# Merging the column-group sums of a sliding-window attention beside a gated feed-forward

## The chip, the cores and the metric

One core of one Trainium2 chip. The metric is device time in microseconds, median of several executions; the profile is one further execution, whose span is some 1.7 us shorter than its device time. The engines are named as the profile names them: PE (TensorE matmuls), PEld (TensorE weight loads), DVE (VectorE), ACT (ScalarE), POOL (GpSimd), SP (the DMA queue's issuer).

Most executions of one kernel agree within 0.3%. Some have a mean granted TensorE clock of 0.992 or 0.993 and take 1.4 to 2.2 us more (the kernel before: 240.2 and 241.7). They widen the intervals. Where I compare single microseconds I therefore go by the medians and, more sharply, by the trace: the stretch from the start of the first projection to the start of the last gating product, which leaves out the loads at the start and the store at the end.

## The reference

```python
xn = layernorm(x)                        # x: 1 x 2048 x 512
q, k, v = split(xn @ wqkv)               # 32 heads of 16
# each position attends to 8 taps: itself and 2, 4, ... 14 positions back
logits[h, s, w] = sum_d q[h, s, d] * k[h, s - 2 w, d] / 4      # -1e9 before position 0
attn = softmax(logits, over w)
o[h, s, d] = sum_w attn[h, s, w] * v[h, s - 2 w, d]
s = o @ wo
g = silu((gelu(xn @ w_gate) * (xn @ w_up)) @ w_down)           # 512 -> 1792 -> 512
out = x + s * g
```

## The kernel before

Sequence positions go in four blocks of 512 columns. For each block TensorE does a feed-forward of 14 steps (`glu`: one gate and one up projection, 8 matmuls of 128 by 128 by 512), 12 projections for the next block (`qkv`) and four `down` steps (14 matmuls of w_down, 4 of wo). Attention runs beside them: VectorE multiplies q with shifted k (`pk`, 8 taps) and the weights with shifted v (`pv`, 8 products), and TensorE sums over partitions. These sums have only 32 output rows, so four of them stand side by side in the array's four groups of 32 columns. Their place in the program is given by hand: `at(("glu", j, 6), f, ...)` runs `f` ahead of step 6 of block j's feed-forward. A bank is the part of TensorE's output memory (PSUM) that one group of sums fills; the banks of a ring are used in turn, each again only when an engine has emptied it.

```python
mm = pool("mm", 5, space=PSUM)     # five banks, a ring for all projections
att = pool("att", 2, space=PSUM)   # two banks for the sums
trp = pool("trp", 1, space=PSUM)   # one bank for transposes

def logits(j, wh):                                  # four of the eight taps
    L = att.tile([P, TQ], F32, tag="att")
    for c in range(NC):
        for wl in range(WL):
            matmul(L[32*wl : 32*(wl+1), :], lhsT=dsum[:, c, :],          # 128 x 32
                   rhs=pk[WL*wh + wl][:, c, :], start=(c == 0), stop=(c == NC-1))
    activation(out=E[:, wh, :], in_=L, func=Exp, scale=SCALE)

def denominators(j):                                # 8 matmuls of 128 x 32, 128 columns
    ...                                             # then rs = reciprocal(den) on VectorE

def spread_reciprocals(j):                          # 4 full-array matmuls, rb = copy on ScalarE
    sp = att.tile([P, TQ], F32, tag="att")
    ...

def av_sum(j, g):                                   # one quarter of the head dimension
    o = att.tile([P, TQ], F32, tag="att")
    for wh in range(WH):
        for i in range(4):
            matmul(o[32*i : 32*(i+1), :], lhsT=hsum, rhs=pv[g, wh][:, i, :],
                   start=(wh == 0), stop=(wh == WH-1))
    tensor_tensor(out=oT[:, g, :], in0=o, in1=rb, op=mult)               # VectorE

# ... cut: the places of the first block
for j in range(1, NJ):
    at(("down", j-1, 3), logits, j, 0)
    at(("glu", j, 1), logits, j, 1)
    at(("glu", j, 2), denominators, j)
    at(("glu", j, 4), spread_reciprocals, j)
    for i in range(8):
        at(("glu", j, 2 + i), av_product, j, i // 2, i % 2)
    for g in range(NC):
        at(("glu", j, 6 + 2*g), av_sum, j, g)
```

The softmax here doesn't subtract the row's maximum and nothing guards it: scores larger than these inputs give would overflow.

## Time and profile before

| | before |
|---|---|
| device time | 240.16 us (240.11 to 240.26, 3 runs) |
| profiled span | 238.2 us |
| TensorE matmuls busy | 229.1 us, 96% of the span |
| share of the chain that ended last | PE 92%, ACT 4% |
| column-group runs (L, den, o) | 4 x (2 + 1 + 4) = 28 |
| table loads on ScalarE | 25 of 1.283 us |
| first projection to last product | 7.96 to 234.26: 226.30 us |

A table load (ACT_TABLE_LOAD) stands in ScalarE's stream wherever gelu, exponential and silu follow one another.

The page is read from the busy shares down: which engine never rests, then whether the chain that ended last is that engine's own. If both say TensorE, only what shortens TensorE's own sequence counts, or what takes away a wait of TensorE. The prediction shows the lines.

### The profile page before, as it was taken

How to read it: one execution, taken by the hardware profiler on the slowest of the kernel's cores; microseconds unless marked ns; L12 is line 12 of the kernel's file. 1: busy time of each engine (PE TensorE's matmuls, PEld its weight loads, DVE VectorE, ACT ScalarE, POOL GpSimd, SP SyncE). 2: the span in 40 equal slices, each digit the busy share in tenths (PEclk: the TensorE clock that was granted, in tenths of full speed). 3: DMA queues.
4: the chain of work that ended last, by engine and by line, in shares of the span. 5: the costliest groups of instructions: out<-in, count | busy, mean ns of one | idle time of the engine just before them, and what ended most of it. 6: DMA issues, size and time to landing. Idle time of an engine off the chain costs nothing.

```text
span 238.2 us, 3516 instructions
## 1 busy us (share of the span) xinstructions
PE 229.1 (96%) x1317; PEld 102.8 (43%) x1342; DVE 143.7 (60%) x222; ACT 150.1 (63%) x237; POOL 24.5 (10%) x80
## 2 busy tenths in 40 slices
PE   7889999999999999999999999999999999999993
PEld 2764444444444343444444444334444434434441
DVE  3559868698488269832537539951347629963131
ACT  2778889976616986568822996656651798566211
POOL 3379922300000000000000000000000000000000
PEclk9999999999999999999999999999999999999999
DMA  6999499610286300000158500000047810000001
GB/s 177 361 373 355 120 198 245 212 45 3 88 198 159 91 0 0 3 0 0 64 132 197 127 20 4 0 0 3 14 128 173 191 31 0 1 3 0 22 22 44
DMA packets 21793, 22.66 MB, mean 95 GB/s; under 512 B 1552, under 2 KB 21776, under 8 KB 21776
## 3 DMA queue, kind: packets, MB, share of 16 engines
q1 hardware_dynamic: 21488, 22.17, 34.8%
q10 hardware_dynamic: 288, 0.26, 0.4%
q8 instruction: 10, 0.16, 0.3%
q14 instruction: 7, 0.06, 0.1%
HBM read 18.22 MB, written 4.21 MB: 94 GB/s over the span
## 4 chain that ended last, share of the span: by engine, by line
PE 92%; ACT 4%; DMA 1%; DVE 1%; issue 1%; POOL 0%; DVEq 0%
PE g_ps L211 20%; PE y_ps L355 20%; PE u_ps L211 19%; PE qkv_ps L211 18%; PE s_ps L366 6%; PE o_ps L326 4%; PE L_ps L265 3%; PE tr L191 1%; ACT xnT L195 1%; DMA x_sb<-in_A_x_dram 1%; ACT ge L345 1%; ACT L345 1%; ACT u L347 0%; PE den_ps L288 0%; PE sp_ps L303 0%
## 5 line engine op out<-in xcount | busy, mean ns | idle before, releaser
L211 PE MATMUL g_ps<-xnT,wg_sb 128*128 128x512 bf16 x218 | 57.4, 380 | 0.5
L211 PE MATMUL u_ps<-xnT,wu_sb 128*128 128x512 bf16 x218 | 56.3, 379 | 0.1
L355 PE MATMUL y_ps<-wd_sb,h 128*128 128x512 bf16 x217 | 50.4, 379 | 0.5 <-issue 0.2
L349 DVE TENSOR_TENSOR h<-ge,u 128x512 bf16<-128x512 bf16 x56 | 23.6, 421 | 37.9 <-ACT u L347 37.5
L211 PE MATMUL qkv_ps<-xnT,wqkv_sb 128*128 128x512 bf16 (+1 forms) x219 | 44.2, 348 | 1.6 <-ACT xnT L195 1.3
L256 DVE TENSOR_TENSOR pk<-q_sb,k_sb 128x2048 bf16<-128x2048 bf16 x32 | 38.0, 1218 | 12.2 <-ACT k_sb L231 12.2
L345 ACT ACTIVATE ge<-g_ps 128x512 bf16<-128x512 f32 x56 | 33.7, 602 | 14.3 <-PE g_ps L211 14.2
L347 ACT ACTIVATE u<-u_ps 128x512 bf16<-128x512 f32 x56 | 33.5, 599 | 12.9 <-PE u_ps L211 11.5
L314 DVE TENSOR_TENSOR pv<-E,v_arr 128x2048 bf16<-128x2048 bf16 x32 | 38.5, 1209 | 0.0
L211 PEld LDWEIGHTS <-wu_sb 128*128 128x128 bf16 x224 | 21.9, 98 | 26.4
L355 PEld LDWEIGHTS <-h 128*128 128x128 bf16 x224 | 21.7, 98 | 27.0 <-issue 1.3
L363 ACT ACTIVATE sl<-y_ps 128x512 bf16<-128x512 f32 x16 | 9.6, 597 | 36.4 <-PE y_ps L355 36.4
L211 PEld LDWEIGHTS <-wg_sb 128*128 128x128 bf16 x224 | 19.9, 98 | 27.5 <-issue 7.2
L211 PEld LDWEIGHTS <-wqkv_sb 128*128 128x128 bf16 x224 | 21.1, 98 | 19.5 <-issue 3.3
L375 DVE TENSOR_TENSOR m<-s_ps,sl 128x512 bf16<-128x512 f32 x16 | 11.1, 692 | 29.5 <-PE s_ps L366 29.5
L366 PE MATMUL s_ps<-wo_sb,oT 128*128 128x512 bf16 x63 | 16.4, 379 | 0.1
L171 DVE BATCH_NORM_STATS2 stats<-x_sb 128x6 f32<-128x512 bf16 x16 | 10.9, 679 | 6.5 <-DMA x_sb<-in_A_x_dram 6.5
L228 ACT ACTIVATE q_sb<-qkv_ps 128x512 bf16<-128x512 f32 (+1 forms) x20 | 10.2, 511 | 4.6 <-PE qkv_ps L211 4.3
L234 ACT ACTIVATE vst<-qkv_ps 128x512 bf16<-128x512 f32 x16 | 9.6, 597 | 5.2 <-PE qkv_ps L211 4.3
L335 DVE TENSOR_TENSOR oT<-o_ps,rb 128x512 bf16<-128x512 f32 x16 | 10.9, 682 | 2.2 <-PE o_ps L326 2.2
L231 ACT ACTIVATE k_sb<-qkv_ps 128x512 bf16<-128x512 f32 (+1 forms) x20 | 10.2, 512 | 3.1 <-PE qkv_ps L211 2.8
L195 ACT ACTIVATE xnT<-tr 128x512 bf16<-128x512 bf16 x16 | 9.5, 597 | 3.7 <-PE tr L191 3.7
(42 smaller groups left out, 135.6 us busy)
## 6 DMA issues: line engine op xcount, KB each, us to landing
v_arr<-vT SPq DMA_DIRECT2D x16, 520.0 KB, 5.4
vT<-vst SPq DMA_DIRECT2D x16, 128.0 KB, 1.7
out_dram<-o_t SPq DMA_DIRECT2D x16, 128.0 KB, 1.8
wg_sb<-in_B_w_gate_dram SPq DMA_DIRECT2D x2, 896.0 KB
wu_sb<-in_B_w_up_dram SPq DMA_DIRECT2D x2, 896.0 KB, 13.1
wd_sb<-in_B_w_down_dram SPq DMA_DIRECT2D x1, 1792.0 KB, 17.4
wqkv_sb<-in_A_wqkv_dram SPq DMA_DIRECT2D x3, 512.0 KB, 6.2
x_sb<-in_A_x_dram SPq DMA_DIRECT2D x3, 512.0 KB, 10.2
```

Source lines behind the costliest of these rows:

```text
L171: nc.vector.bn_stats(out=stats[:, t, :], in_=x_sb[:, t, :])
L195: nc.scalar.activation(out=xnT[j][:, :, i * P : (i + 1) * P], in_=tr[:].rearrange("p (c n) -> p c n", c=NC), func=AF.Copy,)
L211: nc.tensor.matmul(ps[:], lhsT=w[:, dk, lo : lo + P], rhs=xnT[j][:, dk, i0 : i0 + n], start=(dk == 0), stop=(dk == NC - 1),)
L256: nc.vector.tensor_tensor(out=pk[:], in0=st[j]["q"][:], in1=k_sb[:, :, off : off + TQ], op=ALU.mult)
L314: nc.vector.tensor_tensor(out=pv[:], in0=st[j]["E"][:, wh, :].unsqueeze(1).to_broadcast([P, 4, TQ]), in1=st[j]["va"][:, 4 * g : 4 * g + 4, ...
L335: nc.vector.tensor_tensor(out=st[j]["oT"][:, g, :], in0=o[:], in1=st[j]["rb"][:], op=ALU.mult)
L345: nc.scalar.activation(out=ge[:], in_=g_ps[:], func=AF.Gelu_apprx_tanh)
L347: nc.scalar.activation(out=u[:], in_=u_ps[:], func=AF.Copy)
L349: nc.vector.tensor_tensor(out=h[:], in0=ge[:], in1=u[:], op=ALU.mult)
L355: nc.tensor.matmul(y[:], lhsT=st[j][fc][:, tt * P : (tt + 1) * P], rhs=wd_sb[:, fc, :], start=(fc == 0), stop=(fc == NF - 1),)
L366: nc.tensor.matmul(s[:], lhsT=st[j]["oT"][:, g, tt * P : (tt + 1) * P], rhs=wo_sb[:, g, :], start=(g == 0), stop=(g == NC - 1),)
L375: nc.vector.tensor_tensor(out=m[:], in0=s[:], in1=sl[:], op=ALU.mult)
```

## The change

The intent is to give TensorE fewer passages between full-array matmuls and column-group matmuls. All eight taps of the logits go in one run into two neighbouring banks, with one exponential over both; two quarters of the attention sums go in one run into two banks, with one division; the denominators go directly ahead of the first such run. For the banks, transposes and the spread reciprocals move into the general ring.

```diff
-    att = pool("att", 2, space=bass.MemoryType.PSUM)
-    trp = pool("trp", 1, space=bass.MemoryType.PSUM)
+    att = pool("att", 1, space=bass.MemoryType.PSUM)
...
-        tr = trp.tile([P, NC * P], BF16, name="tr")
+        tr = mm.tile([P, NC * P], BF16, name="tr", tag="mm")
...
-    def logits(j, wh):
-        L = att.tile([P, TQ], F32, name="L_ps", tag="att")
+    def logits(j):
+        L = att.tile([P, WH, TQ], F32, name="L_ps", tag="pair")
+        for wh in range(WH):
...
-        nc.scalar.activation(out=E[:, wh, :], in_=L[:], func=AF.Exp, scale=SCALE)
+        nc.scalar.activation(out=E[:], in_=L[:], func=AF.Exp, scale=SCALE)
...
-        den = att.tile([P, P], F32, name="den_ps", tag="att")
+        den = att.tile([P, P], F32, name="den_ps")
...
-        sp = att.tile([P, TQ], F32, name="sp_ps", tag="att")
+        sp = mm.tile([P, TQ], F32, name="sp_ps", tag="mm")
...
-    def av_sum(j, g):
+    def av_sums(j, gg):          # quarters 2*gg and 2*gg + 1, tile [P, 2, TQ], tag "pair"
+    def divide(j, gg):           # one product over [P, 2, TQ]
... (places, blocks 1 to 3; the first block likewise)
-        at(("down", j - 1, 3), logits, j, 0)
-        at(("glu", j, 1), logits, j, 1)
-        at(("glu", j, 2), denominators, j)
-        at(("glu", j, 4), spread_reciprocals, j)
+        at(("glu", j, 0), logits, j)
-        for g in range(NC):
-            at(("glu", j, 6 + 2 * g), av_sum, j, g)
+        at(("glu", j, 7), denominators, j)
+        at(("glu", j, 7), av_sums, j, 0)
+        at(("glu", j, 9), spread_reciprocals, j)
+        at(("glu", j, 9), divide, j, 0)
+        at(("glu", j, 12), av_sums, j, 1)
+        at(("glu", j, 12), divide, j, 1)
...
-            at(("qkv", j, 9 + w) if early else ("down", j - 1, w // 2), qk_product, j, w)
+            at(("qkv", j, 9 + w) if early else ("down", j - 1, w // 3), qk_product, j, w)
```

As the last two lines show, some of VectorE's products move forward as well, so that all eight taps are there for the one run; in the first block so do six of the eight `pv` products.

More of the change, by code (lines that the diff above doesn't have):

```diff
@@ L259, in qk_product @@
         st[j]["pk"][w] = pk
-    def logits(j, wh):
-        L = att.tile([P, TQ], F32, name="L_ps", tag="att")
-        for c in range(NC):
-            for wl in range(WL):
-                nc.tensor.matmul(
-                    L[H * wl : H * (wl + 1), :],
-                    lhsT=dsum[:, c, :],
-                    rhs=st[j]["pk"][WL * wh + wl][:, c, :],
-                    start=(c == 0),
-                    stop=(c == NC - 1),
-                )
-        if wh == 0:
-            st[j]["E"] = ep.tile([P, WH, TQ], BF16, name="E")
-        E = st[j]["E"]
-        nc.scalar.activation(out=E[:, wh, :], in_=L[:], func=AF.Exp, scale=SCALE)
+    def logits(j):
+        L = att.tile([P, WH, TQ], F32, name="L_ps", tag="pair")
+        for wh in range(WH):
+            for c in range(NC):
+                for wl in range(WL):
+                    nc.tensor.matmul(
+                        L[H * wl : H * (wl + 1), wh, :],
+                        lhsT=dsum[:, c, :],
+                        rhs=st[j]["pk"][WL * wh + wl][:, c, :],
+                        start=(c == 0),
+                        stop=(c == NC - 1),
+                    )
+        E = st[j]["E"] = ep.tile([P, WH, TQ], BF16, name="E")
+        nc.scalar.activation(out=E[:], in_=L[:], func=AF.Exp, scale=SCALE)
         if j == 0:
-            for wl in range(WL):
-                w = WL * wh + wl
-                if w:
-                    nc.gpsimd.memset(E[H * wl : H * (wl + 1), wh, 0 : w * DIL], 0.0)
+            for w in range(1, W):
+                wh, wl = divmod(w, WL)
+                nc.gpsimd.memset(E[H * wl : H * (wl + 1), wh, 0 : w * DIL], 0.0)
     def denominators(j):
         E = st[j]["E"]
-        den = att.tile([P, P], F32, name="den_ps", tag="att")
+        den = att.tile([P, P], F32, name="den_ps")
         for wh in range(WH):
@@ L320, in av_product @@
         st[j]["pv"][g, wh] = pv
-    def av_sum(j, g):
-        o = att.tile([P, TQ], F32, name="o_ps", tag="att")
-        for wh in range(WH):
-            for i in range(4):
-                nc.tensor.matmul(
-                    o[H * i : H * (i + 1), :],
-                    lhsT=hsum[:],
-                    rhs=st[j]["pv"][g, wh][:, i, :],
-                    start=(wh == 0),
-                    stop=(wh == WH - 1),
-                )
-        if g == 0:
+    def av_sums(j, gg):
+        o = att.tile([P, 2, TQ], F32, name="o_ps", tag="pair")
+        for g in range(2):
+            for wh in range(WH):
+                for i in range(4):
+                    nc.tensor.matmul(
+                        o[H * i : H * (i + 1), g, :],
+                        lhsT=hsum[:],
+                        rhs=st[j]["pv"][2 * gg + g, wh][:, i, :],
+                        start=(wh == 0),
+                        stop=(wh == WH - 1),
+                    )
+        st[j]["o"] = o
+    def divide(j, gg):
+        if gg == 0:
             st[j]["oT"] = op.tile([P, NC, TQ], BF16, name="oT")
         nc.vector.tensor_tensor(
-            out=st[j]["oT"][:, g, :], in0=o[:], in1=st[j]["rb"][:], op=ALU.mult
+            out=st[j]["oT"][:, 2 * gg : 2 * gg + 2, :],
+            in0=st[j]["o"][:],
+            in1=st[j]["rb"][:].unsqueeze(1).to_broadcast([P, 2, TQ]),
+            op=ALU.mult,
         )
@@ L401 @@
         at(("glu", 0, w), qk_product, 0, w)
-    at(("glu", 0, 6), logits, 0, 0)
-    at(("glu", 0, 10), logits, 0, 1)
-    at(("glu", 0, 12), denominators, 0)
+    at(("glu", 0, 9), logits, 0)
     for i in range(8):
-        at(("glu", 0, 12 + i) if i < 2 else ("qkv", 1, i), av_product, 0, i // 2, i % 2)
-    at(("qkv", 1, 0), spread_reciprocals, 0)
-    for g in range(NC):
-        at(("qkv", 1, 2 + 3 * g), av_sum, 0, g)
+        at(("glu", 0, 12 + i) if i < 2 else ("qkv", 1, (0, 1, 3, 4, 5, 6)[i - 2]),
+           av_product, 0, i // 2, i % 2)
+    at(("qkv", 1, 3), denominators, 0)
+    at(("qkv", 1, 3), av_sums, 0, 0)
+    at(("qkv", 1, 5), spread_reciprocals, 0)
+    at(("qkv", 1, 6), divide, 0, 0)
+    at(("qkv", 1, 10), av_sums, 0, 1)
+    at(("qkv", 1, 10), divide, 0, 1)
     for j in range(1, NJ):
@@ L413 @@
             early = j > 1 and w < 3
-            at(("qkv", j, 9 + w) if early else ("down", j - 1, w // 2), qk_product, j, w)
+            at(("qkv", j, 9 + w) if early else ("down", j - 1, w // 3), qk_product, j, w)
         for i in range(TPQ):
             at(("down", j - 1, i), load_v, j, [i])
-        at(("down", j - 1, 3), logits, j, 0)
-        at(("glu", j, 1), logits, j, 1)
-        at(("glu", j, 2), denominators, j)
-        at(("glu", j, 4), spread_reciprocals, j)
+        at(("glu", j, 0), logits, j)
         for i in range(8):
             at(("glu", j, 2 + i), av_product, j, i // 2, i % 2)
-        for g in range(NC):
-            at(("glu", j, 6 + 2 * g), av_sum, j, g)
+        at(("glu", j, 7), denominators, j)
[4 more added lines that the diff above has]
+        at(("glu", j, 12), divide, j, 1)
     HT = TPQ // 2
```

## The prediction

> **What bounds the kernel now.** I read the page from the top: first the busy shares and the slices, to find the engine that never rests; then the chain that ended last, to see whether that engine also sets the end; then the same chain in order of time for one stretch, to see what one run of column-group sums costs; last the timeline around those runs, to see who feeds them.
>
> ```profile
> PE 229.1 (96%) x1317; PEld 102.8 (43%) x1342; DVE 143.7 (60%) x222; ACT 150.1 (63%) x237; POOL 24.5 (10%) x80
> ...
> PE   7889999999999999999999999999999999999993
> ...
> PEclk9999999999999999999999999999999999999999
> ...
> PE 92%; ACT 4%; DMA 1%; DVE 1%; issue 1%; POOL 0%; DVEq 0%
> PE g_ps L211 20%; PE y_ps L355 20%; PE u_ps L211 19%; PE qkv_ps L211 18%; PE s_ps L366 6%; PE o_ps L326 4%; PE L_ps L265 3%; PE tr L191 1%; ACT xnT L195 1%; DMA x_sb<-in_A_x_dram 1%; ACT ge L345 1%; ACT L345 1%; ACT u L347 0%; PE den_ps L288 0%; PE sp_ps L303 0%
> ```
>
> TensorE is busy in every slice but the first three and the last, at full clock, and 92% of the chain is its own. Nothing off TensorE is worth anything unless TensorE waits for it. The attention sums (L_ps, o_ps, den_ps) are 7 to 8% of the chain, though their arithmetic should be less. The chain in order of time shows why (start, length, piece):
>
> ```profile
> 79.36 0.86 PE u_ps L211 x4
> 80.22 0.98 PE L_ps L265 x16
> 81.20 0.97 PE g_ps L211 x4
> 82.17 0.86 PE u_ps L211 x4
> 83.03 0.23 PE den_ps L288 x8
> ...
> 89.63 0.86 PE u_ps L211 x4
> 90.50 0.55 PE o_ps L326 x8
> 91.04 0.97 PE g_ps L211 x4
> 92.01 0.65 PE u_ps L211 x3
> ```
>
> A group of four full-array matmuls takes 0.86 us, 0.2155 each. A group of four right after a column-group run takes 0.97, so 0.11 more. The column-group run itself, four matmuls side by side, should take 16/4 x 0.2155 = 0.86 for L and 8/4 x 0.2155 = 0.43 for o; it shows 0.98 and 0.55, again 0.11 to 0.12 more. The timeline gives the same from start to start:
>
> ```profile
> 79.20 1.03 PE L211 MATMUL u_ps<-xnT,wu_sb 128*128 128x512 bf16 x4
> 80.15 1.05 PE L265 MATMUL L_ps<-pk,dsum 128*32 128x512 bf16 x16
> 81.13 1.04 PE L211 MATMUL g_ps<-xnT,wg_sb 128*128 128x512 bf16 x4
> 82.01 1.03 PE L211 MATMUL u_ps<-xnT,wu_sb 128*128 128x512 bf16 x4
> 82.96 0.30 PE L288 MATMUL den_ps<-E,hsum 128*32 128x128 bf16 x8
> 83.19 1.04 PE L211 MATMUL g_ps<-xnT,wg_sb 128*128 128x512 bf16 x3
> ...
> 89.47 1.03 PE L211 MATMUL u_ps<-xnT,wu_sb 128*128 128x512 bf16 x4
> 90.43 0.61 PE L326 MATMUL o_ps<-pv,hsum 128*32 128x512 bf16 x8
> 90.97 1.04 PE L211 MATMUL g_ps<-xnT,wg_sb 128*128 128x512 bf16 x4
> ```
>
> Take the start of the group ahead, add 0.86, and read to the start of the group after. L: 81.13 - 80.06 = 1.07, which is 0.86 + 0.21. o: 90.97 - 90.33 = 0.64, which is 0.43 + 0.21. den: 83.19 - 82.87 = 0.32, and its eight matmuls of 128 columns, four side by side, are 2 x 0.054 = 0.11, so 0.21 again. Three lengths, one constant: every run costs 0.21 us whatever is in it, half on entering (0.09 to 0.10), half on leaving (0.11 to 0.12).
>
> **What the Trainium skill says.** "TensorEngine Tiling (Array Packing)", section Key Properties, says that a change of the tiling mode, not of the tile, drains TensorE. The trace agrees and gives the size that the page lacks, 0.21 us for in and out together. "TensorE: Matmul & The Clock Gate", section Back-to-back issue gap, gives 512/2.4 + 2.5 = 216 ns for the isolated warm gap, and 131 ns as sustained; the trace has 215.5 in sustained streams and never 131, so I use 215.5. "ScalarE: Activation LUTs", section What ACT_TABLE_LOAD costs, gives about 1283 ns for a load and 1380 for a drain with it; the trace has 1283 and no such drain: an exponential that starts at 82.17 and lasts 0.60 is followed by a load at 82.78 and by the next gelu at 84.08. "PSUM — Partial Sum Buffer", section Specifications, gives 8 banks of 2 KiB per partition. The program before takes 5 + 2 + 1 of them, and the one after 5 + 2 (the pair) + 1 (the denominators), so the general pool keeps its five but must also serve 16 transposes and 4 spreads.
>
> **The change part by part.**
>
> 1. Runs. Before, each of the four blocks has two L runs, one den run and four o runs: 28 runs. After, one L run and two o runs, with den directly ahead of the first, in the same 128 by 32 tiling and with the same stationary matrix: 12 runs. All 1317 matmuls stay. Sixteen runs less at 0.213 (0.21, and another 0.01 to 0.02 that the first group after a run loses: 81.13 to 82.01 is 0.88 where 0.86 is usual) make 16 x 0.213 = 3.4 us. All of it lies on TensorE in stretches where TensorE never rests, so all of it shows, unless a wait fills it.
>
> 2. Transposes in the general pool. Before, the single transpose buffer makes TensorE wait twice. At the start the second tile's transpose waits 0.57 for the copy of the first; its data are ready at 6.62 (6.21 + 0.41), it runs at 6.89, so with its own bank it gains 0.2, and the first projections hang on the copy after it. In the first feed-forward block the third of the four transposes should start at 22.77 + 0.86 = 23.64 and starts at 23.96, behind a copy that ScalarE reached late because of a table load: 0.3. In the five-bank ring it takes the bank of an already emptied gelu tile (ready at 22.93). Together 0.5 us gained, less certain.
>
> 3. ScalarE. Before, 25 table loads of 1.283 us (9 + 8 + 7 + 1). After, gelu and exponential alternate once per block and silu comes once: 1 + 5 + 4 + 4 = 14. Eleven loads, 14 us of ScalarE, and half of the exponentials' fixed part go. ScalarE is not the bound; I count 0.
>
> 4. VectorE. Sixteen divisions of 682 ns become eight of at most 2 x 0.68 = 1.36 us, spread over two banks. Neutral or slightly better, worth 0 by itself.
>
> 5. Waits that the longer runs may bring. The first o run needs four products instead of two. In later blocks I walked the queue: the exponential ends about 1.1 us after the L run, a gelu load (1.28) and 0.6 follow, so the first products start some 1.3 us after step 2 begins, and products with their gate multiply go at 1.47 us each (88.94 to 90.42), faster than a step of 1.73. The fourth product is there 1.0 us before the run at step 7. The reciprocal comes behind the sixth product and is ready about 1.4 us before the spread at step 9. Second o run: 1.8 us of slack. The first block is tighter. With G the end of its L run, the chain exponential (1.0), load (1.3), gelu and copy (1.1), then VectorE without a pause (8.5 for the remaining gates, normalizations and four products, from the starts 44.50 to 50.04 less the reciprocal and the division in between) gives the fourth product at G + 12.1. TensorE gets to the o run at G + 8.65 (five steps) + 2.8 (three projections and a transpose) = G + 11.5, and to the fourth product's matmuls at G + 12.3. Slack 0.1 to 0.2, an estimate with an error as large; I put 0.1 us of loss on it.
>
> Sum: -3.4 - 0.5 + 0.1 = -3.8; from 240.16 that gives 236.4. Because part 2 is less sure than part 1, I say 236.5.
>
> **The rivals.**
>
> *A: the 0.21 belongs to the matmuls, not to the run.* Then merging saves nothing and the time is about 239.7. Against it: 8 short, 8 long and 16 long matmuls all show the same 0.21. I give it 4%.
>
> *B: a new wait eats the gain.* The first block's four products are the candidate; if my walk is off by 0.7 us, the loss is 0.5 and the time 237.0. A wait in each block, 0.3 to 0.5 us four times, would make it 238. For it: VectorE shows slices of 90% and more around the products. Against it: the reciprocal and two divisions move behind the early products, which frees about 1.5 us ahead of the first run.
>
> *C: the general pool runs dry behind the longer exponential.* After an L run TensorE fills five banks in 0.97 + 4 x 0.86 = 4.4 us; ScalarE returns the first after 1.0 + 1.28 + 0.6 = 2.9 when the exponential's table was loaded during the run, 4.2 when it was not. Before, the same count is 3.6, and no matmul waited. The slack stays positive, with 0.2 us in the worse case; a loss of 0.2 to 0.4 per block would give 237.5.
>
> *D: ScalarE's 14 us show.* Only where TensorE waits for ScalarE, and the waits list has that only for the transposes and in the start, where no load is removed. It could bring the time to 236 but hardly lower.
>
> **Range and chances.** Part 1 is a count times a constant measured three ways, good to 0.2 us; part 2 lies between 0 and 0.7 gained; part 5 between 0 and 1.3 lost. That makes 235.6 to 237.7 for eight in ten. A gain of over 2% needs 235.36 or less, 4.8 us, a microsecond beyond the sum: 6%. A loss over 2% would need 5 us of new waiting with the gain gone as well: 2%. Within 2%: 92%.
>
> **What would show each step.** Right: 12 runs, each with the same 0.21, L runs of about 1.72 + 0.11 in the chain with a following group of 0.97; the first run with den and o in one piece of about 0.97 + 0.11 without 0.11 between them; 14 table loads; the second transpose at about 6.7 us and no gap before the third in the first block; division at 1.2 to 1.4 us. TensorE's busy time then falls by about 3.4 and its idle time by up to 0.5. Wrong: "o_ps waits for pv" in the waits, over 0.5 us in total (rival B); "g_ps or u_ps waits for ge or u" right after an L run (rival C); runs that cost 0.4 (rival A). The number would be wrong first through the first block's o run, where my slack is smaller than my error.

## The result

| | before | after |
|---|---|---|
| device time, median of 6 | 240.28 us | 236.53 us (236.18 to 238.10) |
| ratio | | 0.9839 (0.9801 to 0.9877) |
| profiled span | 238.2 us | 234.4 us |
| PE busy | 229.1 us | 226.7 us |
| ACT busy | 150.1 us | 135.8 us |
| first projection to last product | 226.30 us | 7.54 to 230.45: 222.91 us |

A ratio is the mean time of one kernel's fast runs over that of the other's of the same rounds, so not quite the ratio of the medians. The median fell by 3.75 us. TensorE's busy time is no measure of it here: the trace before holds 1317 of the 1342 matmuls, that after all of them; the prediction took 1317 for the whole count, which none of its sums uses.

The page after, the same rows of the busy shares and of the chain:

```profile
PE 226.7 (97%) x1342; PEld 105.2 (45%) x1342; DVE 143.5 (61%) x214; ACT 135.8 (58%) x222; POOL 26.3 (11%) x80
...
PE 89%; DVE 4%; ACT 3%; issue 1%; DMA 1%; POOL 1%; DVEq 0%; ACTq 0%
```

Still TensorE, but VectorE now holds 4% of the chain. The chain in order of time (start, length, piece) shows the merged runs of the second block and, above them, where VectorE comes in, in the first:

```profile
47.96 2.28 DVE pv L311 x2
50.28 0.40 PE o_ps L325 x4
...
76.08 1.84 PE L_ps L265 x32
...
90.11 0.23 PE den_ps L285 x8
90.34 0.86 PE o_ps L325 x16
91.20 0.97 PE g_ps L210 x4
```

The L run of 32 matmuls takes 1.84, that is 2 x 0.86 + 0.12, where two runs of 0.98 stood. The o run behind the denominators takes 0.86, with nothing of its own for a switch: den has paid. After each run the next full-array group takes 0.97, as before. So there are 12 passages in and out instead of 28, each of the same size. The first two lines are the new wait of the first block: the last four matmuls of its o run start at 50.28, when the fourth product is done.

A second new wait is in the third block. The timeline of the changed kernel, TensorE's rows and then ScalarE's:

```profile
136.73 1.03 PE L210 MATMUL g_ps<-xnT,wg_sb 128*128 128x512 bf16 x4
137.76 1.02 PE L210 MATMUL u_ps<-xnT,wu_sb 128*128 128x512 bf16 x4
...
133.48 1.28 ACT L273 ACT_TABLE_LOAD   x1 [2.22 <-PE L_ps L265]
134.78 1.02 ACT L273 ACTIVATE E<-L_ps 128x1024 bf16<-128x1024 f32 x1
135.82 1.28 ACT L350 ACT_TABLE_LOAD   x1
137.11 0.60 ACT L350 ACTIVATE ge<-g_ps 128x512 bf16<-128x512 f32 x1
```

The up projection would start at 136.73 + 0.86 = 137.59. It starts at 137.76, because the bank it needs is the one whose gelu ends at 137.71. That gelu is late because in this block, and in this one alone, the exponential's table load itself waited for L (2.22 us) instead of running beside it.

### The profile page after: what moved, and what is told of

It reads as the page before. It is cut to its first block, busy times and chain, and to the rows that moved or that the text cites. A ratio compares the mean times of both kernels' runs of the same rounds, so it can differ in the third digit from the quotient of the medians.

```text
span 234.4 us, 3517 instructions
## 1 busy us (share of the span) xinstructions
PE 226.7 (97%) x1342; PEld 105.2 (45%) x1342; DVE 143.5 (61%) x214; ACT 135.8 (58%) x222; POOL 26.3 (11%) x80
## 4 chain that ended last, share of the span: by engine, by line
PE 89%; DVE 4%; ACT 3%; issue 1%; DMA 1%; POOL 1%; DVEq 0%; ACTq 0%
PE y_ps L360 21%; PE g_ps L210 19%; PE u_ps L210 19%; PE qkv_ps L210 17%; PE s_ps L371 6%; PE o_ps L325 3%; PE L_ps L265 2%; DVE pv L311 2%; PE tr L190 1%; DMA x_sb<-in_A_x_dram 1%; ACT ge L350 1%; DVE stats L170 1%; ACT u L352 1%; DVE h L354 1%; POOL rstd L175 1%
## 5 line engine op out<-in xcount | busy, mean ns | idle before, releaser
L210 PE MATMUL u_ps<-xnT,wu_sb 128*128 128x512 bf16 x224 | 57.5, 379 | 0.0
L360 PE MATMUL y_ps<-wd_sb,h 128*128 128x512 bf16 x224 | 51.0, 379 | 0.0
L210 PEld LDWEIGHTS <-wg_sb 128*128 128x128 bf16 x224 | 20.8, 98 | 26.6 <-issue 4.2
L337 DVE TENSOR_TENSOR oT<-o_ps,rb 128x1024 bf16<-128x1024 f32 x8 | 9.8, 1219 | 2.0 <-PE o_ps L325 2.0
```

The source lines that it names most:

```text
L210: nc.tensor.matmul(ps[:], lhsT=w[:, dk, lo : lo + P], rhs=xnT[j][:, dk, i0 : i0 + n], start=(dk == 0), stop=(dk == NC - 1),)
L360: nc.tensor.matmul(y[:], lhsT=st[j][fc][:, tt * P : (tt + 1) * P], rhs=wd_sb[:, fc, :], start=(fc == 0), stop=(fc == NF - 1),)
```

## The experiments

Ten kernels ran, each with five timed rounds against the kernel before and a profile; all gave correct results. The last two, one_run_pre and after_pre, ran on another chip than the eight before them, so they are compared with the others by the stretch and by the kernel before of their own rounds (240.18). "Stretch" is first projection to last product in the trace.

| kernel | runs of column groups | median us | ratio to before (95%) | stretch us |
|---|---|---|---|---|
| before | 28 | 240.28 | 1 | 226.30 |
| after | 12 | 236.53 | 0.984 (0.980 to 0.988) | 222.91 |
| split_all | 28 | 240.73 | 1.003 (1.000 to 1.005) | 227.07 |
| split_fine | 40 | 243.44 | 1.014 (1.011 to 1.017) | 229.71 |
| before_tr_mm | 28 | 239.97 | 1.000 (0.997 to 1.004) | 226.00 |
| late_first | 12 | 237.63 | 0.988 (0.985 to 0.991) | 222.92 |
| ins_full | 20 | 238.48 | 0.990 (0.987 to 0.994) | 224.86 |
| ins_64 | 20 | 238.70 | 0.991 (0.987 to 0.994) | 224.94 |
| ins_32 | 12 | 237.07 | 0.986 (0.982 to 0.990) | 223.25 |
| one_run | 8 | 236.58 | 0.982 (0.979 to 0.986) | 222.90 |
| one_run_pre | 8 | 235.42 | 0.980 (0.977 to 0.984) | 221.93 |
| after_pre | 12 | 236.40 | 0.985 (0.981 to 0.988) | 222.85 |

### split_all: the merged kernel with its runs cut again

```diff
-    at(("glu", 0, 9), logits, 0)
+    at(("glu", 0, 8), logits, 0, (0,)); at(("glu", 0, 9), logits, 0, (1,))
-    at(("qkv", 1, 3), denominators, 0)
-    at(("qkv", 1, 3), av_sums, 0, 0)
+    at(("qkv", 1, 1), denominators, 0); at(("qkv", 1, 2), av_sums, 0, 0, (0,))
+    at(("qkv", 1, 3), reciprocals, 0);  at(("qkv", 1, 3), av_sums, 0, 0, (1,))
... second o run of the first block: halves at qkv 9 and 10
-        at(("glu", j, 0), logits, j)
+        at(("down", j-1, 3), logits, j, (0,)); at(("glu", j, 0), logits, j, (1,))
... blocks 1 to 3: den at 5, o halves at 6 and 7, at 11 and 12; reciprocal stays at 7
```

> The changed kernel with its buffers, its single exponential, its 14 table loads and its divisions of two quarters, but with every merged run cut in two again, so that 28 column-group runs are left, each between full-array matmuls. Theory (0.21 us for each run): 236.5 + 16 x 0.213 - 0.2 (the first block's wait for the fourth product goes) = 239.7 us, 0.997 to 0.999 of the kernel before; TensorE's matmuls no fewer. Rival (the gain comes from the buffers, the table loads or the larger exponentials and divisions): 236.3 to 236.8, so 0.984.

Measured: 240.73 us. With the banks, the 14 table loads and the large exponentials and divisions of the changed kernel, cutting the runs gives the whole gain back: 227.07 - 222.91 = 4.16 us of the stretch, of which the 16 passages are 3.5 and new waits, below, the rest. So the count of runs is the cause, and the 11 saved table loads are worth nothing visible. From the first `down` step on, the three later blocks hold 12 runs more and take 235.32 - 62.61 = 172.71 us against 230.45 - 60.38 = 170.07: 2.64 us, 0.22 for each.

It lost 1.0 us more than I expected. Some 0.1 is the difference between 0.213 and 0.22; the rest lies in the first block. I had expected that block's wait for the fourth product to go (0.2 less); it grew from 0.29 to 0.65 instead (the o half starts at 51.24, the next full group at 52.44: 1.20, where the same half with its exit takes 0.55 elsewhere). The second o run waits 0.20 for the division that empties its two banks (it ends at 58.54, the run starts at 58.59), and an up projection 0.07 for a late gelu (it starts at 43.04). 3.52 - 0.29 + 0.65 + 0.20 + 0.07 = 4.15, so nothing is left over. ScalarE's rows of this kernel and of the changed one show why the first block is late:

```profile
38.76 1.28 ACT L277 ACT_TABLE_LOAD   x1
40.05 1.02 ACT L277 ACTIVATE E<-L_ps 128x1024 bf16<-128x1024 f32 x1
```

```profile
36.94 1.28 ACT L273 ACT_TABLE_LOAD   x1
38.23 1.02 ACT L273 ACTIVATE E<-L_ps 128x1024 bf16<-128x1024 f32 x1
```

The next full group starts at 38.64 in the first and at 37.69 in the second. So the exponential starts 1.41 us behind the short last half, 0.54 behind the long run: while the long run lasts, ScalarE already loads the table. A merged run hides a load that a short one does not, and everything on VectorE follows the exponential.

### split_fine: more runs yet

```diff
+        run("mid", j, fc)        # in glu, between the gate and the up projection
-        at(("glu", j, 6), av_sums, j, 0, (0,))
+        at(("glu", j, 6), av_sums, j, 0, (0,), (0,)); at(("mid", j, 6), av_sums, j, 0, (0,), (1,))
... the same for the other three halves of blocks 1 to 3
```

> As split_all, and the attention sums of blocks two to four cut once more, four matmuls to a run: 40 runs. Theory (a constant for each run, whatever is in it): 12 x 0.213 = 2.6 us more than split_all, 242.3, about 1.008 of the kernel before, and runs of four matmuls take 0.22 + 0.21 = 0.43 us from start to start. Rival (the cost grows with the work in a run): 0.0 to 1.3 us more than split_all.

Measured: 243.44 us, 2.71 more than split_all; in the stretch 229.71 - 227.07 = 2.64, again 0.22 for each of the 12 added runs. The cost is a constant for a run: a run of four matmuls pays as much as one of 32. From where its first matmul would start without a switch (90.68) to the next full group (91.11) such a run takes 0.43, as expected.

### ins_full, ins_64, ins_32: breaking a run with one matmul

```diff
         for wh in range(WH):
+            if wh == 1:
+                matmul(junk[0:COLS, :], lhsT=warm[:, 0:COLS], rhs=warm[:, 0:128])   # COLS = 128, 64, 32
             for c in range(NC):
... and the same between the two quarters of the second o run; junk shares the denominators' bank
```

> The changed kernel with one useless full-array matmul (128 by 128, 128 columns, 0.054 us of its own) in the middle of each L run and of each second o run: 8 insertions that break a run. Theory (the switch of tiling costs, not the neighbour's work): 8 x (0.22 + 0.054) = 2.2 us more than the changed kernel, 238.7. Rival (the constant belongs to the long groups ahead of and behind a run, their weight loads or their waits): 8 x 0.054 = 0.4 us more, 236.9.

> The same with 64 output columns (128 by 64, another column grouping). If a change from groups of 32 to a group of 64 counts as a change of tiling as the skill's page has it: 2.2 us more, 238.7. If all column groupings are one kind and only the whole array is another: 0.4 more, 236.9.

> Control: the same useless matmul in the tiling of the run itself (128 by 32). Both theories: 8 x 0.054 = 0.4 us at most, 236.9, in the trace no 0.1 us gaps inside the run.

The timelines of the second block's L run, first with 128 columns, then with 64:

```profile
76.65 1.05 PE L270 MATMUL L_ps<-pk,dsum 128*32 128x512 bf16 x16
77.63 0.23 PE L265 MATMUL junk<-warm 128*128 128x128 bf16 x1
77.79 1.05 PE L270 MATMUL L_ps<-pk,dsum 128*32 128x512 bf16 x16
```

```profile
76.54 1.05 PE L270 MATMUL L_ps<-pk,dsum 128*32 128x512 bf16 x16
77.52 0.24 PE L265 MATMUL junk<-warm 128*64 128x128 bf16 x1
77.69 1.05 PE L270 MATMUL L_ps<-pk,dsum 128*32 128x512 bf16 x16
```

From the start of the first half to the useless matmul are 0.98 us where the half itself takes 0.86; from it to the second half 0.16, where it takes 0.05. So 0.12 and 0.11 of switching around a single small matmul: long neighbours have no part in it. From the first `down` step on (six insertions), ins_full takes 1.65 us more than the changed kernel, 0.275 for each; ins_64 takes 1.73, 0.29; the control in the run's own tiling takes 0.29, 0.05. What is left for the switch is 0.22 to 0.24 in the first two. A change from groups of 32 to one of 64 columns costs the same as a change to the whole array. "TensorEngine Tiling (Array Packing)", section Key Properties, says that the mode, not the tile, is what drains; these three runs agree.

What the switch is made of shows in part in the weight loads (PEld). Within a tiling, a matmul's weights load while the matmul ahead of it runs: in ins_32 the useless matmul's weights start to load at 77.123, 0.214 before the matmul itself. At a change of tiling they do not. This is the load ahead of the second block's denominators in the changed kernel:

```profile
90.04 0.12 PEld L285 LDWEIGHTS <-hsum 128*32 128x32 bf16 x8 [0.42 <-issue]
```

The load starts together with its matmul, 0.309 us after the last full-array matmul (89.732) where 0.2155 is usual: 0.093 more, and one such load takes 0.093. On leaving (91.13) it is 0.096, and the load there takes 0.096. So of the 0.22 some 0.19 are as long as two weight loads that nothing hides. Whether the loads are the cost, or only wait for the same thing as the matmuls, no run here separates.

In the first block the insertion into L was largely paid by the wait there: in ins_full the run with the denominators starts at 49.87 and the next projection at 50.98, 1.11 us, with no wait left in it, and up to the first `down` step that kernel lost 0.3 us instead of 0.55.

### before_tr_mm: only the transposes moved

```diff
-    trp = pool("trp", 1, space=bass.MemoryType.PSUM)
-        tr = trp.tile([P, NC * P], BF16, name="tr")
+        tr = mm.tile([P, NC * P], BF16, name="tr", tag="mm")
```

> The kernel before with one thing of the change: transposes in the general pool of five banks, the single transpose buffer gone, 28 runs as before. Theory: the second transpose runs 0.2 us earlier after its data and the first feed-forward block loses its wait of 0.3: 240.2 - 0.5 = 239.7, ratio 0.998. In the trace the third transpose of that block follows its predecessor with no gap. Rival (later waits absorb it, or the general pool runs dry): 240.2 or more, with a new wait of g_ps or u_ps on ScalarE.

Measured: 239.97 us, by the interval nothing (two of its six runs had the low clock; the other four lie at 239.46 to 240.28, with a median of 239.6, where the kernel before without its low-clock run has 240.26: in the direction expected, but four runs are few). The trace is sharper: the stretch is 226.00 against 226.30. The third transpose of the first feed-forward block, before and with this edit:

```profile
22.77 1.03 PE L211 MATMUL u_ps<-xnT,wu_sb 128*128 128x512 bf16 x4
23.96 0.38 PE L191 MATMUL tr<-ident,xn 128*128 128x128 bf16 x4 [0.16 <-DVE h L349]
```

```profile
23.37 1.03 PE L210 MATMUL u_ps<-xnT,wu_sb 128*128 128x512 bf16 x4
24.23 0.39 PE L190 MATMUL tr<-ident,xn 128*128 128x128 bf16 x4
```

1.19 us from one start to the other before, 0.86 after: the wait of 0.3 is gone, as predicted. (The profile names VectorE as what ended it; the copy on ScalarE that empties the bank ends at 23.90.) The 0.2 at the start is another matter. The second transpose does come earlier, but in this run the first projection then waits 1.24 us, till 8.54, for the weights' load; in eight of the eleven kernels profiled with the transposes in the ring it waits for that load, and it starts at 7.77 to 8.54 in the ten experiments, 7.54 in the one profile of the changed kernel, 7.96 in that of the kernel before. The earlier copy only helps in executions where the load is early. How often that is, these runs do not settle.

### late_first: the first block's sums one projection later

```diff
-    at(("qkv", 1, 3), denominators, 0)
-    at(("qkv", 1, 3), av_sums, 0, 0)
-    at(("qkv", 1, 5), spread_reciprocals, 0)
-    at(("qkv", 1, 6), divide, 0, 0)
+    at(("qkv", 1, 4), denominators, 0)
+    at(("qkv", 1, 4), av_sums, 0, 0)
+    at(("qkv", 1, 6), spread_reciprocals, 0)
+    at(("qkv", 1, 7), divide, 0, 0)
```

> The changed kernel with the first block's denominators, first sums, spread and division one projection later. Theory: the wait of the first run for its fourth product (1.38 us from start to start where 1.18 is the run and its switch) goes, and nothing else moves: 236.5 - 0.2 = 236.3; in the trace the run with the denominators takes 1.18. Rival: the later division delays the second run or the first s sums, and the time stays or rises by 0.2.

Measured: a stretch of 222.92, no gain at all (its median of 237.63 is that of three runs with the low clock; the other three lie at 236.36 to 237.10). The chain tells where the wait went:

```profile
48.92 4.54 DVE pv L311 x4
53.46 0.88 DVE rs L294
54.38 0.40 PE sp_ps L300 x4
```

The run itself now takes 1.09 us from start to start, without a wait; I had expected 1.18, so the wait that it lost was 0.29 and not 0.2. But VectorE's queue now has the sixth product ahead of the reciprocal as well, so the reciprocal ends at 54.34, and the spread, due at about 54.1, waits for it. VectorE is 0.3 us behind TensorE at this place in both orders that were tried. My rival had named the wrong wait.

### one_run and one_run_pre: all of a block's attention sums at once

```diff
-    mm = pool("mm", 5, ...)          att = pool("att", 1, ...)
+    mm = pool("mm", 4, ...)          att = pool("att", 2, ...)      # two pairs; den from the ring
-        at(("glu", j, 7), denominators, j);  at(("glu", j, 7), av_sums, j, 0)
-        at(("glu", j, 9), spread_reciprocals, j);  at(("glu", j, 9), divide, j, 0)
-        at(("glu", j, 12), av_sums, j, 1);  at(("glu", j, 12), divide, j, 1)
+        at(("glu", j, 11), denominators, j);  at(("glu", j, 11), av_sums, j, gg)      # gg = 0, 1
+        at(("glu", j, 13), spread_reciprocals, j);  at(("glu", j, 13), divide, j, gg)
... first block: qkv 8 and 10
```

> One step beyond the change: the denominators and all 32 matmuls of a block's attention sums in one run into four banks (two pairs), the denominators' bank from the general pool, which goes from five banks to four: 8 runs instead of 12. Theory: 4 x 0.22 less, and the first block's 0.2 of waiting for its fourth product goes: 236.5 - 0.9 - 0.2 = 235.4, ratio 0.980. Rival (four banks are too few behind the exponential, where the fifth matmul group would have to wait for a gelu that comes 3.2 to 3.5 us after the L run, against 3.55 of work in four banks): waits of 0.1 to 0.5 us per block, 235.8 to 237.5, with g_ps or u_ps waiting for ScalarE.

Measured: 236.58 us, no better than the changed kernel, though four passages are gone. A wait in the third block took most of the gain:

```profile
133.38 1.28 ACT L273 ACT_TABLE_LOAD   x1 [2.24 <-PE L_ps L265]
137.66 1.02 PE L210 MATMUL g_ps<-xnT,wg_sb 128*128 128x512 bf16 x4 [0.89 <-ACT ge L350]
```

It is the late table load that already cost the changed kernel 0.17; with a ring of four the bank is wanted one group earlier, 0.86 us, and the same lateness costs 1.06: the u group ahead starts at 135.74, so 136.60 was due (the 0.89 of the view counts from the modelled end of that group). In the first block a ring of four costs two smaller waits, each behind a table load: 0.21 for a projection that starts at 22.90, which with five banks does not wait, and 0.06 at 41.75. The stretch adds up: -0.88 for four passages, -0.29 and -0.17 for the two waits of the changed kernel, + 1.06 + 0.21 + 0.06 = -0.01. So the rival, four banks too few, was right in three places. Against the largest I put a one-column exponential of a constant on ScalarE ahead of each L run, which brings the table in time:

```diff
     def logits(j):
+        nc.scalar.activation(out=pre[:], in_=mhalf[:], func=AF.Exp)      # 128 x 1
```

> one_run with a one-column exponential of a constant put on ScalarE ahead of each L run, so that the table load is done before the L run ends also in the third block, where it had waited 2.2 us for L and then held a general bank 0.89 us too long. Theory (that single wait ate the gain of one_run): 0.9 less than one_run, 236.6 - 0.9 = 235.7, ratio 0.979, no wait of g_ps for ge in the trace, and from the first projection to the last product 222.0 instead of 222.9 us. Rival (four banks are too few elsewhere as well, or the extra exponential delays the gelus): 236.2 or more.

> The changed kernel with the same early exponential. Theory: only the 0.16 us that the third block's second up-projection waits (137.76 instead of 137.60) goes: 236.5 - 0.16 = 236.3, in the trace 222.75 instead of 222.91 from first projection to last product. Rival: no change, or the extra instruction costs as much.

ScalarE in the third block of one_run_pre:

```profile
131.13 1.28 ACT L263 ACT_TABLE_LOAD   x1
132.43 0.20 ACT L263 ACTIVATE pre<-mhalf 128x1 f32<-128x1 f32 x1
133.38 1.02 ACT L276 ACTIVATE E<-L_ps 128x1024 bf16<-128x1024 f32 x1 [0.74 <-PE L_ps L268]
```

The load now lies beside the L run; the wait of the gate projection is gone. The two waits of the first block stay (0.21 and 0.15), so four banks remain a little too few. One_run_pre takes 235.42 us, 1.16 less than one_run, with a stretch of 221.93 against the 222.0 expected, 0.97 less than one_run's. It is the fastest kernel, 4.76 us under the kernel before of its own rounds (240.18). In the changed kernel the same instruction brings the 0.16 expected in the third block, whose up projection starts at 138.64, 0.87 after the gate projection at 137.77. It costs 0.11 in the first: there the exponential starts 1.40 us after its table load (37.90 to 39.30) instead of 1.29 (36.94 to 38.23), because the small one stands between them, and the run with the denominators takes 1.47 instead of 1.38. So my rival was nearly right: 236.40, stretch 222.85, a gain of 0.06 that the times do not resolve.

## Why the prediction was right

Predicted 236.5, measured 236.53, in the range of 235.6 to 237.7. That the sums agree to 0.03 is partly luck. The mechanism, a constant for each passage, held. But within the stretch I had predicted 3.4 + 0.3 - 0.1 = 3.6, and 3.39 came: two losses were larger than I had them, the gain of the runs slightly larger too. The medians fell by 0.36 more than the stretch, outside it, at the start or the end of the executions, where I had predicted 0.2 and where only the profiled execution can be read. The terms are these.

- **Runs, step 1.** Predicted 16 x 0.213 = 3.4 us. Shown by split_all and split_fine: 0.22 for each of 12 and of 12 runs, so 3.5. Rival A, that the constant belongs to the matmuls, fell with split_fine and with the single inserted matmul.
- **Transposes, step 2.** Predicted 0.3 in the first feed-forward block and 0.2 at the start. The 0.3 is shown by before_tr_mm. The 0.2 at the start comes only where the weights are early: in the changed kernel's profile the first projection follows the first transpose by 1.96 us (5.58 to 7.54), before by 2.15 (5.81 to 7.96), but in eight of the eleven profiles it waits for its weights, which the step had overlooked. That profile starts its projections 0.42 earlier than the one before; the other 0.23 was there at the first transpose, whose start lies between 5.58 and 5.91 in the twelve profiles.
- **ScalarE, step 3.** Predicted 14 table loads, worth 0. There are 14, and split_all, which keeps them, has no gain left. Rival D fell with it.
- **VectorE, step 4.** Predicted at most 1.36 us for a division; it takes 1.219, against 682 ns for one of half the size.
- **Waits, step 5.** Predicted a loss of 0.1 in the first block from a slack of 0.1 to 0.2. The run with the denominators takes 1.38 us from start to start (49.24 to 50.62) where late_first has 1.09 for it: a loss of 0.29. The term that was too small is the exponential's start. I had let it begin as the L run ends; it begins 0.54 later, when its table load ends. VectorE's own part was right (8.5 predicted, 41.68 to 50.24 measured), though rival B's 1.5 us is the reciprocal and one division (0.87 + 0.60), not two. For the later blocks the walk held: no wait of o for a product in any of them.
- **Rival C.** I had counted 4.2 us till the first bank is free when the table is not loaded during the run, against 4.4 of work, a slack of 0.2 in the worse case. That case occurred, once, and cost 0.17. The idea was right, the margin wrong by 0.3 to 0.4: waiting for L, the load starts 0.2 us after the next group has begun, where I had let everything start at once, and five groups are 4.3 us of work, not 4.4 (133.27 to 137.59).

Sum: -3.52 - 0.30 + 0.29 + 0.17 = -3.36 us; the stretch fell by 226.30 - 222.91 = 3.39. In the profile's span the start adds 0.42, which gives 3.8.

Why the table load waits for L in the third block and not in the others can be read in the packed trace, which keeps the semaphores that each instruction waits for (the timeline leaves instructions that only wait out). In the second and fourth blocks of the changed kernel the exponential waits for TensorE alone; it carries this wait itself, and the load ahead of it starts freely. In the third it also waits for GpSimd, which in the first block writes zeros into E, a ring of two buffers. There the wait for L is an instruction of its own (133.44), ahead of the load (133.48). The kernel before has the same at 130.85 and 130.90, a wait of 1.30 us, so it is not the change's doing; in one_run_pre that instruction (133.31) comes behind the load (131.13). In the first block the exponential has two waits as well, but the separate one, for VectorE (37.84), comes behind the load (36.94). That the zeros bring the second wait is read from the program and was not tested by a run.

Open are what brings the low clock in some executions, and what a switch of tiling consists of beyond the lengths above.

## What to carry to other kernels

Where TensorE never rests, count the passages between tilings: each run of narrow matmuls cost its constant for going in and out here, so make runs few and long and put narrow sums of the same tiling next to each other. Then ask of each longer run what it must have before it can start and which bank is wanted first behind it; one table load at the wrong moment ate in one_run more than four passages had gained (1.06 against 0.88). A gain of a per cent is easier read as a difference between two marks within a trace than from medians, because the start of an execution varies by as much.

## What the Trainium skill lacked or had wrong

- "TensorEngine Tiling (Array Packing)", Key Properties, says that a change of tiling mode drains TensorE but gives no size. Here going in and out costs 0.22 us together, for runs of 4, 8, 16 and 32 matmuls alike, 0.09 to 0.11 on each side, and a change from 128 by 32 to 128 by 64 and back costs as much as one to the whole array (0.24 and 0.22). Nor does the page give a measured case of what goes on without a drain: the denominators (128 columns) ahead of the o sums (512) cost no second passage, and a matmul with another stationary matrix in the tiling of the run cost 0.05 us, its own length.
- "TensorE: Matmul & The Clock Gate", Back-to-back issue gap, gives 131 ns for a sustained 512-column matmul beside its weight loads. The streams here go at 215.5 ns, the page's isolated figure.
- "ScalarE: Activation LUTs", What ACT_TABLE_LOAD costs, adds a drain of some 1380 ns to the load of 1283. The loads here take 1283 and the next activation starts some 10 ns behind them (load at 135.82, gelu at 137.11). No page says that a load may stand behind the wait of the activation that it serves: that held it up by 2.2 us in one block of four, and a one-column activation ahead (0.20 us of ScalarE) put it in time.
